# One assignment product per block with both centroid parts, first-unit maxima of three heads as b + relu(a - b), duplicates on GpSimd, and a new order

## The chip, the cores and the metric

One core of a Trainium2 chip runs the kernel. The metric is the device time of one execution in microseconds (us). The engines are TensorE (PE; its weight loads are listed as PEld), VectorE (DVE), ScalarE (ACT), GpSimd (POOL) and SyncE (SP), which issues DMAs.

## What is computed

Clustered attention for 4 batches x 8 heads x 768 tokens of 64 dimensions, with its output fed to a mixture of experts with greedy, capacity-limited routing. Cut to what matters here:

```python
q_assign = np.argmax(np.einsum('bhsd,hcd->bhsc', q_n, c_n), axis=-1)   # 16 centroids per head
k_assign = np.argmax(np.einsum('bhsd,hcd->bhsc', k_n, c_n), axis=-1)
mask = q_assign[:, :, :, None] == k_assign[:, :, None, :]
scores = scale * np.matmul(q, k.transpose(0, 1, 3, 2))
scores = np.where(mask, scores, -1000000000.0)
scores = scores - np.max(scores, axis=-1, keepdims=True)
attn = np.exp(scores); attn = attn / (np.sum(attn, axis=-1, keepdims=True) + 1e-09)
out = np.matmul(attn, v)                                               # then _moe_ref(x = out)
```

## The kernel before

Attention runs over eight units, `u = 0..7`; a unit is one batch and four heads, and has 24 blocks of 128 tokens (six per head). All inputs are held as two float16 parts, high and low, so that float16 products give nearly float32 precision. A unit goes through these steps, whose names stand in the order:

- `load`, `split_sc`, `split_hi`, `split_lo`: inputs arrive by DMA and are split into parts; `dup` copies the high parts into a second layout (`qb`, `kb`); `trans` (DMA) or `pt` and `ptc` (TensorE and a copy, first unit only) transpose the blocks into `qat`, `kat`, `qbt`, `kbt`.
- `cent` (L666) multiplies each block of queries or keys with the 16 centroids of its head, through `assign` (L655): for each block a product with the centroids' high part and one with their low part, 16 columns each, added up in a PSUM tile of the pool `pmx`. `hot0` to `hot5` make the one-hot marks of the nearest centroid from it. For the first unit `cent0` and `hh0` to `hh5` do the same, a head at a time.
- `m_mm` (L770): for a block of 128 queries the scores against the 768 keys of the head, high parts and marks alone, two products of 384 columns (L774); `m_rd` (L777) takes the maximum of each row on VectorE, one 128x768 reduction (L778). `row0` to `row2` put the maxima into `qbt`.
- `b_mm` (L812): the full scores, transposed, four products of 384 columns (L813, L817); `b_exp` (L819) the exponential on ScalarE; `res` (L825) the low part of the exponential, on GpSimd (letter P) or VectorE (D).
- `av` (L840): the value products, three for each of six query blocks, 66, 64 and 66 columns (L850, L852, L831). One PSUM tile of the pool `pav` holds a head's sums; `out0`, `out1`, `out2` scale it (L860, L863, L871), `hi0` and `hi1` split the result (L879, L883), and only then may the next head's `av` start. In the second block of a head come six products with the mean of the values (L856).

`m_mm` of unit u + 1, `cent` of unit u + 2 and `b_mm` and `av` of unit u run interleaved. The PSUM pool `psc` has three buffers of two banks, which `m_mm`, `b_mm` and `pt` share; `pmx` and `pav` have one each.

The program is unrolled, and the string `ATT_ORDER` says in which order its steps are issued: each entry is a step's name and its arguments (`m_rd,3,16` is the row maximum of block 16 of unit 3). Each engine takes its instructions in this order. `wd` is a filler product, which keeps TensorE occupied at the start. A second string orders the mixture of experts.

## Time and profile before

| | |
|---|---|
| time, median of 3 runs | 678.08 us (677.74 to 678.26) |
| profiled execution: time | 679.02 us |
| profiled execution: span | 677.2 us, mean granted clock 0.979 |
| busy in the span: TensorE, VectorE, ScalarE, GpSimd | 651.9, 506.6, 422.2, 484.9 us |

The span is the time from the first to the last instruction of the program; the time of the execution contains some more around it. Busy times are unions of an engine's instructions. TensorE's matmuls are pipelined, so each is listed longer than the step from one to the next: the step is read from the starts.

### The profile page before, as it was taken

How to read it: one execution, taken by the hardware profiler on the slowest of the kernel's cores; microseconds unless marked ns; L12 is line 12 of the kernel's file. 1: busy time of each engine (PE TensorE's matmuls, PEld its weight loads, DVE VectorE, ACT ScalarE, POOL GpSimd, SP SyncE). 2: the span in 40 equal slices, each digit the busy share in tenths (PEclk: the TensorE clock that was granted, in tenths of full speed). 3: DMA queues.
4: the chain of work that ended last, by engine and by line, in shares of the span. 5: the costliest groups of instructions: out<-in, count | busy, mean ns of one | idle time of the engine just before them, and what ended most of it. 6: DMA issues, size and time to landing. Idle time of an engine off the chain costs nothing. (4 is left out here: it accounts for less than half of the span.)

```text
span 677.2 us, 19763 instructions
## 1 busy us (share of the span) xinstructions
PE 651.9 (96%) x8286; PEld 436.9 (65%) x8286; DVE 506.6 (75%) x1157; ACT 422.2 (62%) x555; POOL 484.9 (72%) x389
## 2 busy tenths in 40 slices
PE   7999999999999999999999879999999999999996
PEld 5657777776777777777777559554545454545453
DVE  6898999999998989998887666877768585822020
ACT  8886676585767767565554046749494847598121
POOL 6568889899798877977774447677695949499301
PEclk9999999999999999999999569999999999999999
DMA  6887889776987979572223043729474766696101
GB/s 190 198 193 174 156 157 228 111 178 149 189 195 128 170 183 136 98 141 54 52 51 73 26 172 126 296 80 319 152 244 189 199 242 163 260 310 177 46 1 47
DMA packets 175451, 105.86 MB, mean 156 GB/s; under 512 B 135426, under 2 KB 160002, under 8 KB 175362
## 3 DMA queue, kind: packets, MB, share of 16 engines
q1 hardware_dynamic: 171378, 91.81, 56.7%
q0 software_dynamic: 3840, 12.59, 4.9%
q8 instruction: 65, 1.06, 0.6%
q10 hardware_dynamic: 144, 0.20, 0.1%
q14 instruction: 24, 0.20, 0.1%
HBM read 58.77 MB, written 12.58 MB: 105 GB/s over the span
## 5 line engine op out<-in xcount | busy, mean ns | idle before, releaser
L828 POOL TENSOR_TENSOR rt<-pt 128x768 f16<-128x768 f32 x176 | 267.2, 1544 | 63.5 <-ACT pt L820 63.3
L820 ACT ACTIVATE pt<-sc 128x768 f32<-128x768 f32 x192 | 150.6, 811 | 102.1 <-PE sc L817 99.2
L778 DVE TENSOR_REDUCE mxs<-sc 128x1 f32<-128x768 f32 x192 | 178.8, 951 | 12.7 <-PE sc L774 11.0
L1426 PE MATMUL pf<-xgt,w1h 128*128 128x384 f16 (+1 forms) x640 | 128.8, 293 | 0.3 <-DVE xgt L738 0.3
L850 PE MATMUL av<-vh,pt 128*128 128x66 f16 x1152 | 121.7, 194 | 0.1
L831 PE MATMUL av<-vh,rt 128*128 128x66 f16 x1152 | 121.4, 193 | 0.0
L852 PE MATMUL av<-vl,pt 128*128 128x64 f16 x1152 | 121.4, 191 | 0.0
L850 PEld LDWEIGHTS <-pt 128*128 128x128 bf16 x1152 | 106.0, 97 | 8.3
L852 PEld LDWEIGHTS <-pt 128*128 128x128 bf16 x1152 | 105.5, 98 | 8.5 <-issue 0.5
L831 PEld LDWEIGHTS <-rt 128*128 128x128 f16 x1152 | 104.7, 97 | 0.0
L813 PE MATMUL sc<-qbt,kbt 99*128 99x384 f16 x384 | 93.8, 325 | 1.1 <-DMA qbt<-mt 0.4
L817 PE MATMUL sc<-qat,kat 128*128 128x384 f16 x384 | 93.7, 325 | 0.0
L774 PE MATMUL sc<-kbt,qbt 80*128 80x384 f16 x384 | 90.2, 325 | 1.7 <-ACT qbt L736 0.6
L1426 PE MATMUL pf<-xgt,w1l 128*128 128x384 f16 (+1 forms) x320 | 90.0, 293 | 0.0
L1388 ACT ACTIVATE wr<-wr 128x1024 f32<-128x1024 f32 x64 | 66.8, 1046 | 26.4 <-DMA wr<-in_moe_w_dram 26.3
L1426 PEld LDWEIGHTS <-w1h 128*128 128x128 f16 x640 | 57.3, 97 | 28.7 <-issue 1.1
L1464 PE MATMUL pf<-w2h,hh 128*128 128x512 f16 x184 | 69.6, 378 | 0.0
L1464 PE MATMUL pf<-w2h,hl 128*128 128x512 f16 x184 | 69.4, 378 | 0.0
L1464 PE MATMUL pf<-w2l,hh 128*128 128x512 f16 x184 | 69.4, 378 | 0.0
L1398 POOL TENSOR_TENSOR w2l<-wr,w2h 128x1024 f16<-128x1024 f32 x32 | 67.6, 2134 | 1.9 <-ACT w2h L1391 1.6
L1398 POOL TENSOR_TENSOR w1l<-wr,w1h 128x1024 f16<-128x1024 f32 x32 | 67.6, 2138 | 0.2
L1402 POOL DMA_INDIRECT xg<-xrow,idx x24 | 23.3, 972 | 57.7 <-DVE idx L1361 20.6
(253 smaller groups left out, 1158.5 us busy)
## 6 DMA issues: line engine op xcount, KB each, us to landing
wr<-in_moe_w_dram SPq DMA_DIRECT2D x64, 512.0 KB
ld<-in_v_dram SPq DMA_DIRECT2D x8, 768.0 KB
xrow<-xb SPq DMA_DIRECT2D x16, 384.0 KB
ld<-in_k_dram SPq DMA_DIRECT2D x7, 768.0 KB
...
xg<-xrow,idx POOLq DMA_INDIRECT x24, 6.0
```

Of the source, the lines that this page charges most:

```text
L774: nc.tensor.matmul(p[:, half, :S // 2], QBT[u][:D + C, i, :], KBT[u][:D + C, h * J + half * 3:h * J + half * 3 + 3, :], start=True, stop=True)
L778: nc.vector.tensor_reduce(mxs[u % 3][:, i:i + 1], MP.pop((u, i))[:, :, :S // 2], axis=AX.XY, op=OP.max)
L813: nc.tensor.matmul(ps[:, half, :S // 2], KBT[u][:ER + 3, s, :], QBT[u][:ER + 3, cs, :], start=True, stop=False)
L817: nc.tensor.matmul(ps[:, half, :S // 2], KAT[u][:, s, :], QAT[u][:, cs, :], start=False, stop=True)
L820: nc.scalar.activation(pts[(u * 12 + s // 2) % RP][:, s % 2], MP.pop((u, "b", s))[:, :, :S // 2], AF.Exp, scale=ESC)
L828: (nc.vector if e == "D" else nc.gpsimd).tensor_sub(rts[x][:, s % 2], p.rearrange("p a b -> p (a b)"), hi_view(pts[x])[:, s % 2])
L831: nc.tensor.matmul(o[:, j, :], r[:, j * P:(j + 1) * P], VH[u][:, s, :], start=False, stop=(s % J == J - 1), skip_group_check=True)
L850: nc.tensor.matmul(o[:, j, :], hi[:, js], VH[u][:, s, :], start=(kt == 0 and j == 0), stop=False, skip_group_check=True)
L852: nc.tensor.matmul(o[:, j, :D], hi[:, js], VL[u][:, s, :], start=False, stop=False, skip_group_check=True)
L1398: nc.gpsimd.tensor_sub(lo, wrs[c], hi)
L1426: nc.tensor.matmul(o, (w1l if i == 2 else w1h)[x][:, c, fs], xgt[x][:, h + int(i == 1), ts], start=(first and i == 0), stop=(last and i == ...
L1464: nc.tensor.matmul(PS["o", p, g], (hl if i == 2 else hh)[x][:, f, g * P:(g + 1) * P], (w2l if i == 1 else w2h)[x][:, f, :], start=(f == 0 ...
```

## The change

1. `cent` issues one product for each block, 32 columns, against both parts of the centroids at once, into a tile of `psc`. The two results are added afterwards: `small` (`hotb` in the order) copies the low part's results to `cb` on ScalarE, and `both` (`hota`) adds the high part's to it on VectorE, into the tile of `pmx`. This holds for units 1 to 7, queries and keys; `cent0` stays.
2. In unit 0 the maxima of heads 1 to 3 (18 blocks) are made otherwise. `kd` subtracts the second half of a head's keys from the first; the first of the two products then gives a - b, where a and b are the scores against the two halves. `m_rl` takes relu(a - b) on ScalarE, and `m_rd` adds b and takes the maximum in one instruction of VectorE over 384 columns.
3. Six of the duplications of unit 0 run on GpSimd. The chain that normalises the centroids (`c2`) has ten steps instead of sixteen.
4. Value products write 65 columns instead of 66.
5. `ATT_ORDER` is new. As many fillers stand in it as before. The order of the mixture of experts is unchanged.

```diff
@@ -19,169 +19,174 @@
 ATT_ORDER = """
...
+m_rd,3,0 b_mm,2,10 row2,2,1 m_mm,3,1 out0,2,0 b_exp,2,10 cent,4,k,0 out1,2,0 cent,4,k,1 m_rd,3,1 cent,4,k,2 tab,11
+xtr,1,1 cent,4,k,3 res,2,7,P m_mm,3,2 hotb,4,k out2,2,0,D b_mm,2,11 hota,4,k hi0,2,0 res,2,9,P m_rd,3,2 b_exp,2,11
...
     def cent(u, name, h):
         if h == 0:
+            PC["w", name] = psc.tile([P, T, 2, C], F32, name="sc")
+        if h == 1:
             PC[name] = pmx.tile([P, T, C], F32, name="mx")
-        assign(PC[name][:, h * J:(h + 1) * J], (QAT if name == "q" else KAT)[u], u % NG, h, h == 0)
+        o, src, g = PC["w", name], (QAT if name == "q" else KAT)[u], u % NG * HG + h
+        for j in range(h * J, (h + 1) * J):
+            nc.tensor.matmul(o[:, j], src[:, j, :], ct[:, :, g * C:(g + 1) * C], start=(j % 16 == 0), stop=True,
+                             skip_group_check=True)
+
+    def small(u, name):
+        nc.scalar.activation(cb, PC["w", name][:, :, 1], AF.Copy)
+
+    def both(u, name):
+        nc.vector.tensor_tensor(PC[name], PC.pop(("w", name))[:, :, 0], cb, op=OP.add)
...
-            nc.tensor.matmul(p[:, half, :S // 2], QBT[u][:D + C, i, :],
-                             KBT[u][:D + C, h * J + half * 3:h * J + half * 3 + 3, :], start=True, stop=True)
+            x = KBT[u][:D + C, h * J + half * 3:h * J + half * 3 + 3, :]
+            if paired(u, i) and half == 0:
+                x = kdv(h)
+            nc.tensor.matmul(p[:, half, :S // 2], QBT[u][:D + C, i, :], x, start=True, stop=True)
+
+    def paired(u, i):
+        return u == 0 and i >= 1 * J
...
+    def kd(u, h):
+        k = KBT[u][:D + C, h * J:(h + 1) * J, :]
+        nc.vector.tensor_sub(kdv(h), k[:, 0:3], k[:, 3:6])
+
+    def m_rl(u, i):
+        nc.scalar.activation(rlv(i), MP[u, i][:, 0, :S // 2], AF.Relu)
...
-        nc.vector.tensor_reduce(mxs[u % 3][:, i:i + 1], MP.pop((u, i))[:, :, :S // 2], axis=AX.XY, op=OP.max)
+        o, p = mxs[u % 3][:, i:i + 1], MP.pop((u, i))
+        if paired(u, i):
+            nc.vector.tensor_tensor_reduce(rlv(i), p[:, 1, :S // 2], rlv(i), 1.0, LOWEST,
+                                           op0=OP.add, op1=OP.max, accum_out=o)
+        else:
+            nc.vector.tensor_reduce(o, p[:, :, :S // 2], axis=AX.XY, op=OP.max)
...
-            nc.tensor.matmul(o[:, j, :], hi[:, js], VH[u][:, s, :], start=(kt == 0 and j == 0), stop=False,
+            nc.tensor.matmul(o[:, j, :D + 1], hi[:, js], VH[u][:, s, :D + 1], start=(kt == 0 and j == 0), stop=False,
```

The instructions' order at two places. First VectorE, where unit 2's first head ends and unit 4's keys are assigned; before the change (`rc`, `av`, `xb` are the scaling and splitting of the head's sums, `mxs` row maxima of unit 3, `cmx` the first step of the marks):

```order
L778 TENSOR_REDUCE mxs_140<-sc 128x1
L860 TENSOR_SCALAR rc<-av 128x6
L863 RECIPROCAL rc<-rc 128x6
L871 TENSOR_TENSOR av<-av,rc 128x6x64
L778 TENSOR_REDUCE mxs_140<-sc 128x1
L883 TENSOR_TENSOR xb_146<-av,xb_146 128x6x64
L778 TENSOR_REDUCE mxs_140<-sc 128x1 x2
L679 TENSOR_REDUCE cmx<-mx 128x24
```

After it, where `mx<-sc,cb` (L691) is the sum of the two parts:

```order
L824 TENSOR_REDUCE mxs_140<-sc 128x1
L906 TENSOR_SCALAR rc<-av 128x6
L909 RECIPROCAL rc<-rc 128x6
L824 TENSOR_REDUCE mxs_140<-sc 128x1
L917 TENSOR_TENSOR av<-av,rc 128x6x64
L691 TENSOR_TENSOR mx<-sc,cb 128x384
L824 TENSOR_REDUCE mxs_140<-sc 128x1
L929 TENSOR_TENSOR xb_146<-av,xb_146 128x6x64
L824 TENSOR_REDUCE mxs_140<-sc 128x1
L701 TENSOR_REDUCE cmx<-mx 128x24
```

A row maximum now stands between L909 and L917, and the sum between L917 and the next maximum, so L929, the last step of the head's sums, is two instructions further from the first.

Second ScalarE, around its first exponential (`pt<-sc`, behind a table load); before (`vh` is a part of unit 1's values, `qb` and `kb` with 24x64 its duplicates and with 24x16 its marks, `kb` with 6x16 marks of unit 0, `qbt` transposed blocks of unit 0):

```order
L638 ACTIVATE vh_107<-ld_76 128x24x64
L695 ACTIVATE kb<-ceq 128x6x16
L736 ACTIVATE qbt_118<-sc 128x768
L736 ACTIVATE qbt_118<-sc 3x768
L650 ACTIVATE qb<-qa 128x24x64
L820 ACT_TABLE_LOAD
L820 ACTIVATE pt_127<-sc 128x768
L695 ACTIVATE kb<-ceq 128x24x16
L652 ACTIVATE kb<-ka 128x24x64
```

After, where L816 is a relu of unit 0 and L688 the copy of the low part's results of unit 1's queries:

```order
L816 ACTIVATE xt_149<-sc 128x384
L661 ACTIVATE qb<-qa 128x24x64
L758 ACTIVATE qbt_118<-sc 3x768
L816 ACTIVATE xt_148<-sc 128x384
L816 ACTIVATE xt_149<-sc 128x384
L688 ACTIVATE cb<-sc 128x384
L816 ACTIVATE xt_148<-sc 128x384
L717 ACTIVATE kb<-ceq 128x24x16
L816 ACTIVATE xt_149<-sc 128x384
L663 ACTIVATE kb<-ka 128x24x64
L866 ACT_TABLE_LOAD
L866 ACTIVATE pt_127<-sc 128x768
```

Four relus and a copy now stand between the duplicate of unit 1's queries and the table load, and unit 1's marks and duplicate of the keys moved ahead of the first exponential.

## Rows read from the trace of the kernel before

**Rows 1.** Five stretches: busy time, instructions, clock, DMA share, GB/s.

```profile
core 0: us, PE busy (x) PEld busy (x) DVE busy (x) ACT busy (x) POOL busy (x), PEclk, DMA share, GB/s
0.00:18.50 18.50, 14.54 (x139) 9.07 (x140) 12.11 (x43) 15.65 (x27) 13.40 (x36) 1.00 0.59 175
18.50:51.40 32.90, 30.75 (x351) 20.63 (x348) 30.85 (x52) 28.36 (x38) 19.66 (x10) 1.00 0.89 204
51.40:306.30 254.90, 251.94 (x4393) 191.25 (x4392) 238.69 (x388) 170.24 (x222) 216.88 (x161) 1.00 0.80 160
306.30:370.30 64.00, 64.00 (x1155) 48.83 (x1153) 51.88 (x90) 36.15 (x52) 44.84 (x31) 1.00 0.28 55
370.30:677.20 306.90, 290.63 (x2260) 167.15 (x2256) 173.05 (x588) 171.82 (x219) 190.13 (x153) 0.95 0.52 168
```

**Rows 2.** Groups by line, TensorE, 0 to 51.4: busy, mean ns, idle before.

```profile
L664 PE MATMUL av<-onesh 128*128 128x384 f16 x91 | 22.4, 360 | 1.5 <-POOL onesh L572 1.5
```

**Rows 3.** Waits of TensorE, 51.4 to 306.3: total us, times, longest.

```profile
PE mx L657 <- DVE L L954: 1.4, 2, 1.0
```

**Rows 4.** Waits of VectorE, 51.4 to 306.3.

```profile
DVE mxs L778 <- PE sc L774: 6.7, 16, 0.9
DVE xb L883 <- ACT xb L879: 2.2, 5, 0.7
```

**Rows 5.** Timeline of TensorE at a head boundary: start, us, instruction.

```profile
188.72 0.49 PE L774 MATMUL sc<-kbt,qbt 80*128 80x384 f16 x2
189.06 0.49 PE L813 MATMUL sc<-qbt,kbt 99*128 99x384 f16 x2
...
189.71 0.75 PE L657 MATMUL mx<-ct,kat 128*128 128x16 f16 x24
190.31 0.48 PE L774 MATMUL sc<-kbt,qbt 80*128 80x384 f16 x2
...
192.22 0.19 PE L850 MATMUL av<-vh,pt 128*128 128x66 f16 x1
```

**Rows 6.** Timeline of VectorE at the same boundary.

```profile
189.26 0.15 DVE L860 TENSOR_SCALAR rc<-av 128x6 f32<-128x6 f32 x1
...
189.67 0.57 DVE L871 TENSOR_TENSOR av<-av,rc 128x384 f32<-128x384 f32 x1
190.15 0.95 DVE L778 TENSOR_REDUCE mxs<-sc 128x1 f32<-128x768 f32 x1
191.01 0.55 DVE L883 TENSOR_TENSOR xb<-av,xb 128x384 f16<-128x384 f32 x1
191.48 0.95 DVE L778 TENSOR_REDUCE mxs<-sc 128x1 f32<-128x768 f32 x1
```

**Rows 7.** Timeline of TensorE in the second half: a 32-column product.

```profile
443.20 0.31 PE L1202 MATMUL pc<-oh,ind 128*128 128x32 bf16 x6
```

**Rows 8.** Timeline of TensorE: value products, first and last of ten.

```profile
196.37 0.19 PE L850 MATMUL av<-vh,pt 128*128 128x66 f16 x1
...
196.64 0.19 PE L850 MATMUL av<-vh,pt 128*128 128x66 f16 x1
```

**Rows 9.** Groups by line and shape, VectorE, 0 to 374.

```profile
L828 DVE TENSOR_TENSOR rt<-pt 128x768 f16<-128x768 f32 x16 | 15.8, 999 | 3.4 <-ACT pt L820 3.3
...
L528 DVE TENSOR_TENSOR ss<-ss 128x1 f32<-128x1 f32 x4 | 0.6, 160 | 0.1
```

**Rows 10.** Groups by line and shape, VectorE, 372 to 450: compare with accumulator.

```profile
L1236 DVE TENSOR_SCALAR_CACHE_REDUCE scr<-pc 32x8 bf16<-32x8 f32 x12 | 1.9, 156 | 3.6 <-PE pc L1230 2.0 <-PE pc L1196 1.5
...
L1236 DVE DVE_READ_ACCUMULATOR scr<-pc 32x1 bf16 x12 | 0.9, 74 | 0.0
```

**Rows 11.** Groups by line and shape, ScalarE, 0 to 374.

```profile
L879 ACT ACTIVATE xb<-av 128x384 f16<-128x384 f32 x32 | 15.6, 488 | 11.7 <-DVE av L871 8.7 <-PE sc L817 2.4 <-issue 0.3
...
L650 ACT ACTIVATE qb<-qa 128x384 f16<-128x384 f16 x4 | 2.0, 511 | 0.0
```

**Rows 12.** Groups by line and shape, GpSimd, 0 to 374.

```profile
L645 POOL TENSOR_TENSOR ka<-ld,ka 128x384 f16<-128x384 f32 x3 | 2.7, 917 | 3.3 <-ACT ka L638 3.3
...
L569 POOL MEMSET qm<- 128x600 f16 x1 | 0.6, 600 | 0.0
```

More of the change, by code (lines that the diff above doesn't have):

```diff
@@ L182 @@
[L182 to L184 removed]
+load,0,q,0,A ones tab,0 wd ident split_hi,0,q,0,D tab,4 wd load,0,k,0 tab,10 wd zqb loadc wd load,0,q,1 wd wd load,0,k,1
+zkb wd load,0,q,2 wd load,0,k,3 wd wd split_hi,0,k,0,D load,0,k,2 misc wd c0 dup,0,k,0 load,0,v,- wd c1 load,0,q,3 wd
@@ new lines @@
+av,0,1 m_rl,0,21 m_mm,0,22 vact,1 m_rd,0,20 res,0,6,P av,0,2 vh2,1 trans,2,ka,- m_rd,0,21 m_rl,0,22 b_mm,0,7 m_rd,0,22
+av,0,3 b_exp,0,7 row0,0,2 res,0,4,D m_mm,0,23 pt,0,qm,2 m_rl,0,23 b_mm,0,8 res,0,7,P ptc,0,qm,2,A m_rd,0,23 av,0,4 vl2,1
+b_exp,0,8 m_mm,1,0 load,2,v,- m_mm,1,1 split_hi,2,q,-,D m_rd,1,0 b_mm,0,9 res,0,8,P load,3,q,- av,0,5 m_rd,1,1 b_mm,0,10
+b_exp,0,9 out0,0,0 row1,0,3 row0,0,3 out1,0,0 m_mm,1,2 tab,1 out2,0,0,D b_exp,0,10 res,0,9,P cent,2,k,0 cent,2,k,1
+cent,2,k,2 m_rd,1,2 cent,2,k,3 hi0,0,0 b_mm,0,11 hotb,2,k hi1,0,0 res,0,10,P m_mm,1,4 hota,2,k b_exp,0,11 av,0,6
@@ new lines @@
+m_rd,1,9 av,0,13 split_hi,2,v,-,D m_mm,1,12 hot4,2,k res,0,18,P av,0,14 m_rd,1,10 b_mm,0,19 hot5,2,k m_rd,1,12 av,0,15
+b_exp,0,19 b_mm,0,20 row0,1,0 row1,1,0 split_lo,2,v,-,D split_hi,3,k,-,D rowt,1,0 b_mm,0,22 m_mm,1,13 av,0,16 b_exp,0,20
+m_rd,1,13 res,0,19,P av,0,17 b_exp,0,22 lg0,0,0 out0,0,2 row2,1,0 m_mm,1,14 out1,0,2 lg1,0,0 cent,2,q,0 out2,0,2,D
+res,0,20,P cent,2,q,1 cent,2,q,2 load,4,k,- cent,2,q,3 m_rd,1,14 hi0,0,2 b_mm,0,23 trans,2,kb,- hotb,2,q b_mm,0,21
+b_exp,0,23 tab,3 hi1,0,2 res,0,22,P hota,2,q av,0,18 b_exp,0,21 hot0,2,q m_mm,1,15 av,0,19 tab,2 hot1,2,q res,0,21,P
@@ new lines @@
+split_hi,3,q,-,D m_rd,1,22 b_mm,1,7 vl2,2 av,1,3 b_exp,1,7 row0,1,1 row1,1,1 b_mm,1,8 split_lo,3,q,-,D rowt,1,1 av,1,4
+b_exp,1,8 av,1,5 m_mm,2,0 res,1,7,P out0,1,0 b_mm,1,9 out1,1,0 m_rd,2,0 row2,1,1 m_mm,2,1 b_exp,1,9 res,1,8,P m_rd,2,1
+b_mm,1,10 load,4,v,- xst,0,0 m_mm,2,2 out2,1,0,D b_exp,1,10 cent,3,k,0 cent,3,k,1 trans,3,qa,- cent,3,k,2 m_rd,2,2
+res,1,6,P cent,3,k,3 hi0,1,0 b_mm,1,11 hotb,3,k hi1,1,0 m_mm,2,4 hota,3,k b_exp,1,11 res,1,10,P av,1,6 m_rd,2,4
+split_hi,3,v,-,D m_mm,2,6 m_mm,2,3 m_rd,2,6 b_mm,1,13 res,1,9,P av,1,7 hot0,3,k b_exp,1,13 m_rd,2,3 av,1,8 res,1,11,P
@@ new lines @@
+row2,3,1 b_mm,3,10 out0,3,0 m_rd,4,1 cent,5,k,0 load,6,k,- cent,5,k,1 b_exp,3,10 cent,5,k,2 res,3,6,P cent,5,k,3
+out1,3,0 xst,2,0 b_mm,3,11 out2,3,0,D hotb,5,k trans,5,qa,- m_mm,4,2 hi0,3,0 hota,5,k b_exp,3,11 res,3,7,P hi1,3,0
+m_mm,4,4 m_rd,4,2 b_mm,3,13 res,3,8,P m_rd,4,4 m_mm,4,6 b_exp,3,13 av,3,6 m_rd,4,6 dup,5,k,- m_mm,4,3 av,3,7 res,3,10,P
+hot0,5,k av,3,8 m_rd,4,3 b_mm,3,12 res,3,11,P hot1,5,k m_mm,4,5 b_exp,3,12 av,3,9 m_rd,4,5 b_mm,3,14 res,3,13,P
+load,6,v,- hot2,5,k b_mm,3,15 b_exp,3,14 load,6,q,- hot3,5,k m_mm,4,7 res,3,12,P b_exp,3,15 av,3,10 hot4,5,k m_mm,4,9
@@ new lines @@
+xst,3,0 m_mm,5,2 hota,6,k hi0,4,0 res,4,8,P trans,6,qa,- b_exp,4,10 m_rd,5,2 b_mm,4,11 m_mm,5,3 hi1,4,0 b_exp,4,11
+m_mm,5,4 res,4,9,P m_rd,5,3 av,4,6 dup,6,k,- av,4,7 m_rd,5,4 res,4,10,P b_mm,4,12 hot0,6,k m_mm,5,6 b_exp,4,12 av,4,8
+m_rd,5,6 b_mm,4,13 res,4,12,P hot1,6,k m_mm,5,5 b_exp,4,13 b_mm,4,14 hot2,6,k m_rd,5,5 res,4,11,P m_mm,5,7 b_exp,4,14
+av,4,9 hot3,6,k b_mm,4,15 m_rd,5,7 res,4,13,P av,4,10 b_exp,4,15 m_mm,5,9 hot4,6,k av,4,11 m_rd,5,9 res,4,15,P b_mm,4,16
+load,7,k,- out0,4,1 m_mm,5,8 out1,4,1 b_exp,4,16 out2,4,1,D b_mm,4,17 res,4,14,P m_rd,5,8 hi0,4,1 lg0,3,1 b_mm,4,18
@@ L185 @@
+bb,1,9 bb,1,4 bb,1,10
 """
```

350 lines of the change are left out of this document (168 added, 182 removed).

## The prediction

> **What bounds the kernel now.** I read the stretches first: busy time of each engine in five parts of the span, cut at the first row-maximum product (18.5 us), the first value product (51.4), the first value product of the seventh unit (306.3) and the last value product (370.3). The reader is to see [rows 1] that from 51.4 to 306.3 TensorE is busy 251.9 of 254.9 us and VectorE 238.7, so TensorE is the limit with VectorE close behind (16.2 us free); that from 306.3 to 370.3 TensorE is busy throughout and VectorE has 12 us free; and that behind 370.3 lies the mixture of experts, which the change does not touch. Before 51.4 it is otherwise: 91 of TensorE's products there are fillers that compute nothing [rows 2], 91 x 0.16 = 14.7 us of array time at the step of a 384-column product (0.33 us for two, [rows 5]). TensorE waits there for the data that VectorE and ScalarE prepare; between 18.5 and 51.4 they are busy 30.9 and 28.4 of 32.9 us [rows 1].
>
> Then the waits. In the long stretch TensorE's longest named wait adds up to 1.4 us [rows 3], while VectorE waits 6.7 us for row-maximum products alone [rows 4]. So there a product taken from TensorE shortens the kernel, as long as VectorE, which gets work, does not use up its slack.
>
> **Term 1, the assignment products.** Each of 14 groups (queries and keys of units 1 to 7) has 24 blocks; before, two 16-column products with a weight load each, 48 in all; after, 24 products of 32 columns. The timeline shows 24 of the old in 0.60 us, start to start (189.71 to 190.31, [rows 5]), 25 ns each, so 48 take 1.20 us. A 32-column product with a weight load exists in the second half: six last 0.31 us together and one 0.177, so (0.31 - 0.177) / 5 = 27 ns a step [rows 7]. 24 x 25 or 27 ns is 0.60 or 0.64 us: a group saves 0.56 to 0.60, and I take 0.60. Unit 1's two groups lie in the start, where TensorE has fillers to spare: nothing. The other 12 lie between 51.4 and 306.3: **-7.2 us** (bounds -6.7 and -7.2).
>
> **Term 2, 65 columns for 66.** Two of three value products and the 192 with the means lose a column: 2 x 1152 + 192 = 2496 products. Nine value products, three of each kind, take 0.27 us (196.37 to 196.64, [rows 8]), so 90 ns for 66 + 64 + 66 columns: the step follows the columns, with some 3 ns on top. The granted clock is 1.00 up to 370.3 [rows 1], the upper of the two levels, 2.4 GHz, and a column is 0.42 ns: **-1.0 us**. No row has an odd width, so the bounds are -1.0 and nothing, and I could not exclude a loss of the same size; I take -1.0, since nothing in the rows makes parity matter.
>
> **Term 3, what VectorE gets.** Each group now needs a sum of the two parts (hota) on VectorE, 128x384 of float32 from PSUM. The nearest rows are the scaling and the low part of the output, also 128x384: 0.57 and 0.55 us long, the next instruction 0.48 and 0.47 us behind their start [rows 6]. Twelve in the long stretch: 12 x 0.47 = 5.6 us. In front of it stands a copy on ScalarE (0.49 us, [rows 11]), which is busy 170 of 254.9 us there and hides it; but the sum waits for the copy. Four of the new maxima also lie in this stretch and give back 4 x 0.3 (below). The order moves some steps across the stretch's ends (a split in; a residual, a maximum and short ones out), by my estimate -1.7 us. VectorE then has 238.7 + 5.6 - 1.2 - 1.7 = 241.4 us of work in a stretch that TensorE could pass in 254.9 - 8.0 = 246.9: 5.5 us free where it had 16.2.
>
> The price is paid at the head boundaries. There the one accumulator for values must be read out (out0, out1, out2, copy, hi1) before the next head's products start. Before, out0 to hi1 with one row maximum between ran from 189.26 to about 191.56, 2.3 us [rows 6], while TensorE had 3.50 us of other products (188.72 to 192.22, [rows 5]); assignment products were 1.2 us of that. The VectorE excerpt of the order shows one more maximum (0.86 us) and the sum (0.47) inside this chain: 3.6 us, and with the 0.5 us between TensorE's last value product and out0 (188.72 to 189.26) 4.1. The new order lays beside it two score blocks (2 x 0.65, 189.06 to 189.71), five pairs of maximum products (5 x 0.33) and 0.60 of assignment products, together 3.55 us. So 0.5 us of waiting there. Also the products of a group now sit in one of the three score buffers until the sum is done, where before they sat in a buffer of their own. The other boundaries in the order are better covered, so I take 0.2 us for each of the 12, between nothing and the whole 0.6 that it saved: **+2.4 us** (0 to 7.2).
>
> **Term 4, the start.** The 18 new maxima: a step of a 951 ns maximum is 0.86 us (190.15 to 191.01, [rows 6]). The new one reads half as much: between 0.47 (the 128x384 step) with 0.09 for reading the accumulator, 0.56, if it goes like the sums, and 0.86, no gain. A compare with accumulator lasts 0.156 and its read 0.074 [rows 10], so the read is cheap, and I take 0.56: 18 x 0.30 = 5.4 us off VectorE. Six small steps of the centroid chain go as well, 0.16 us each [rows 9], 1.0 us. Against that VectorE gets two sums (0.9), three differences of keys (80x384, at most 0.5 each: 1.4) and three residuals that GpSimd made (0.99 each, [rows 9]: 2.6 at the step of a maximum). Sum: -5.4 - 1.0 + 0.9 + 1.4 + 2.6 = -1.5 us. ScalarE gets 18 halves for the relu and two copies, some 0.49 us each [rows 11]: +9.8, and loses six duplications of 0.51 [rows 11]: -3.1. In the ScalarE excerpt of the order relus stand in front of the first exponential. The six duplications on GpSimd take between 0.6 (a fill of 600) and 0.92 us (a 128x384 subtraction) each [rows 12]; GpSimd is busy 33 of the first 51.4 us [rows 1] and covers them. So ScalarE, busy 44 of the first 51.4 us, gets about 6.7 us that it has little room for, and VectorE loses 1.5. The start may be shorter by 1.5 or longer by 2; I take **0**.
>
> **Sum.** -7.2 - 1.0 + 2.4 + 0 = -5.8 us. The profiled execution took 679.0 us, a span of 677.2 and 1.8 around it, 0.9 above the median of 678.1. Counted from the median: **672.3 us**.
>
> **Rivals.**
> - *Everything is hidden and the start gets shorter.* VectorE's named waits in the long stretch [rows 4] then shrink without touching TensorE: -8.2, and -1.5 from the start: 668.4. For it speaks that TensorE lost only 3 us in the stretch with VectorE busy 94%; against it that the slack falls to a third.
> - *VectorE takes over the bound, and the kernel is slower.* Place: 51.4 to 306.3. If VectorE stays idle as long as now, 16.2 us, because its waits come from the chain through TensorE and ScalarE and not from spare time, the stretch takes 241.4 + 16.2 = 257.6, 2.7 us more than now; less 0.2 for the columns in the last stretch: 680.6. It decides from 13.5 us of idle time on (254.9 - 241.4). Against it: much of that idle time was waiting for TensorE [rows 4], which now comes sooner. The Trainium skill bears on this ("VectorE: DVE Perf Modes", section "The DRAIN you can't avoid"): the next operation does not start until the pipe is empty. By that the sums would cost their whole 0.57 us, 6.8 instead of 5.6, and 4.3 us would stay free. The rows differ: the maximum of 190.15 lasts 0.95 us and the next instruction starts at 191.01, 0.09 us before its end, so I count steps.
> - *The new maximum is dear.* If its step is over 0.56 + 5.8 / 18 = 0.88 us, the start gives back all the rest: 678 at 0.88, 680 at 1.0. No row shows this instruction.
> - *The wider product does not halve the time,* because a group spread over two banks of PSUM steps slower: at 50 ns a product term 1 is nothing, and 678.1 - 1.0 + 2.4 is 679.5. The 27 ns of [rows 7] speak against it.
>
> **Chances.** The forecast 0.58; the first rival 0.17; VectorE's bound 0.12; the dear maximum 0.10; the last 0.03. A measurement of this kernel can tell about 0.2%, 1.4 us, from no change. The first two cases are faster throughout; of the next two, half lies above the bound, a third within it and the rest below. So faster 0.79, same 0.10, slower 0.11. Range: from 667.5, a little beyond the first rival, to 678.5, which leaves out the slower half of the two dear cases.
>
> **What would show it.** In the changed kernel's trace: assignment products at 25 to 27 ns a step; nine value products in under 0.27 us; the long stretch 249 us instead of 254.9, with TensorE idle about 5 us and VectorE 8; the new maximum with its read under 0.6 us a step; the first value product near 51 us. I am wrong if VectorE is idle over 13 us in that stretch, if a score product waits over 0.5 us for the buffer at each group, or if the first value product comes after 54 us.

## The result and the profile after

The changed kernel is slower: median 683.38 us (681.30 to 685.48, 8 runs) against 678.77 for the kernel before beside it (677.74 to 681.75, 8 runs), ratio 1.0067 with an interval of 1.0048 to 1.0086. The forecast was 672.3. The profiled execution took 685.48 us, a span of 683.7 at a mean granted clock of 0.971 (before: 677.2 and 0.979). It is the slowest of the eight: its trace shows 6.5 us more than the trace of before, where the medians differ by 4.6, and what the other seven had less of is not recorded.

The same five stretches as in [rows 1], cut at the same events of the changed kernel's trace (first row-maximum product 21.7, first value product 59.9, seventh unit 311.1, last value product 377.0). Two of the cuts of [rows 1] are not quite what they are called: the first row-maximum product of the kernel before starts at 17.55 and the one at 18.5 is the second block's, so that the first one now comes 4.1 us later; and both cuts at the last value product lie 0.7 us ahead of the very last ones (371.0 and 377.7).

```profile
0.00:21.70 21.70, 15.17 (x138) 9.34 (x139) 11.94 (x34) 13.52 (x23) 14.85 (x42) 0.84 0.58 184
21.70:59.90 38.20, 32.21 (x302) 20.64 (x303) 30.58 (x77) 33.27 (x50) 17.63 (x12) 0.96 0.70 158
59.90:311.10 251.20, 247.88 (x4104) 184.09 (x4102) 238.01 (x397) 178.80 (x239) 219.72 (x155) 1.00 0.80 160
311.10:377.00 65.90, 64.69 (x1158) 49.05 (x1156) 52.68 (x92) 36.45 (x52) 46.97 (x35) 1.00 0.24 58
377.00:683.70 306.70, 290.47 (x2260) 167.10 (x2256) 172.73 (x588) 171.92 (x219) 189.92 (x153) 0.95 0.52 168
```

The first value product comes at 59.9 instead of 51.4 us: the start loses 8.5 us, and its clock column shows 0.84 and 0.96 where it showed 1.00. From the first to the last value product it takes 317.1 instead of 318.9 us, a gain of 1.8 where 5.8 were forecast. The mixture of experts is 0.2 us shorter. 8.5 - 1.8 - 0.2 = 6.5 us, the difference of the two spans.

**The start.** Stretch by stretch (columns as in [rows 1]; the third number from the end is the clock):

```profile
5.70:9.40 3.70, 0.36 (x6) 0.35 (x6) 2.34 (x10) 3.62 (x8) 3.10 (x11) 1.00 1.03 365
9.40:16.20 6.80, 4.74 (x49) 3.22 (x47) 4.87 (x11) 2.53 (x6) 5.90 (x10) 0.50 0.51 148
16.20:36.70 20.50, 17.86 (x231) 12.43 (x230) 16.99 (x43) 17.57 (x26) 11.25 (x7) 1.00 0.57 127
36.70:40.10 3.40, 3.40 (x27) 2.30 (x24) 1.95 (x6) 2.87 (x4) 0.00 (x0) 0.50 0.99 171
40.10:59.90 19.80, 16.36 (x125) 9.78 (x124) 15.95 (x40) 17.13 (x26) 7.47 (x5) 1.00 0.70 182
```

For 10.2 us in two stretches TensorE runs at the lower level, 1.2 GHz; the kernel before shows 1.00 in every stretch up to its last value product [rows 1]. Ahead of the first fall TensorE had nothing to do (its timeline; the number in brackets is the idle time before the row):

```profile
5.15 0.52 PE L675 MATMUL av<-onesh 128*128 128x384 f16 x1
9.04 0.52 PE L754 MATMUL sc<-ident,ka 128*128 128x128 f16 x6 [3.37 <-DVE ss L534]
```

L675 is the last of the 14 fillers that the new order puts ahead of the first transposition of keys; one more stands between it and the copy of the centroids (`c4`). The order before had 11 and 9 there. Ahead of the second fall are two idle times of 1.04 and 0.93 us, at 33.1 and 35.2.

**Short VectorE steps that end with a GpSimd instruction.** VectorE's timeline at the end of the centroid chain, and GpSimd's at the same time:

```profile
9.01 0.86 DVE L534 TENSOR_SCALAR sq<-cf,ss 128x64 f32<-128x64 f32 x1
9.90 1.00 DVE L534 CAST cst<-sq 128x128 f16<-128x128 f32 x1
...
10.94 0.91 DVE L534 TENSOR_TENSOR cst<-sq,cst 128x128 f16<-128x128 f32 x1
```

```profile
8.91 0.91 POOL L652 TENSOR_TENSOR ka<-ld,ka 128x384 f16<-128x384 f32 x1
9.78 0.91 POOL L652 TENSOR_TENSOR qa<-ld,qa 128x384 f16<-128x384 f32 x1
10.63 0.20 POOL L1032 MEMSET wdig<- 128x128 bf16 x1
10.79 0.91 POOL L652 TENSOR_TENSOR qa<-ld,qa 128x384 f16<-128x384 f32 x1
```

The first ends at 9.87, the GpSimd instruction beside it at 9.82; the third at 11.85 and 11.70. In the kernel before, with GpSimd idle there, the first took 0.26 us, and the other two, half as wide (128x64), 0.19 and 0.22. The longest is the second copy of the first head's maxima:

```profile
39.31 0.16 DVE L842 TENSOR_SCALAR qm<-mxs 128x12 f16<-128x12 f32 x1
40.13 0.56 DVE L760 COPY kbt<-sc 128x768 f16<-128x768 f16 x1 [0.66 <-PE sc L754]
40.61 2.88 DVE L838 TENSOR_SCALAR qm<-mxs 128x12 f16<-128x12 f32 x1
```

```profile
40.48 2.98 POOL L652 TENSOR_TENSOR vl<-ld,vh 128x1536 f16<-128x1536 f32 x1 [6.03 <-ACT vh L645]
```

Two steps of the same shape: 0.16 us with GpSimd idle, 2.88 us beside a GpSimd instruction that ends at 43.46. The Trainium skill ("GPSIMD Engine Reference", section "Key points") says that GpSimd shares its SBUF interfaces with VectorE, and names as contending those VectorE instructions that run in a two-port mode or have two SBUF inputs. The trace agrees for the second kind: the step of 10.94 us, with two inputs in SBUF, was held, and the new maximum of 54.11 us, with one operand in PSUM, ran its usual 0.56 us beside a GpSimd residual of 53.77 to 55.23. In which mode the held steps with one input ran, no view shows.

**The long stretch.** One group of assignment products in TensorE's timeline, and the new maximum in VectorE's:

```profile
278.48 0.75 PE L684 MATMUL sc<-ct,kat 128*128 128x32 f16 x24
279.18 0.48 PE L859 MATMUL sc<-qbt,kbt 99*128 99x384 f16 x2
```

```profile
46.00 0.55 DVE L821 CUSTOM_DVE_ANT_0 xt<-sc,xt 128x384 f32<-128x384 f32 x1
46.47 0.08 DVE L821 DVE_READ_ACCUMULATOR2_ANT mxs<- 128x1 f32 x1
46.47 0.55 DVE L821 CUSTOM_DVE_ANT_0 xt<-sc,xt 128x384 f32<-128x384 f32 x1
```

The 24 products take 0.60 us (0.70 start to start, of which 0.10 is a wait for the next score buffer), a new maximum 0.47 with its read beside the next one. The named waits of TensorE in 59.9 to 311.1 still look small:

```profile
PE sc L684 <- DVE mxs L824: 1.1, 1, 1.1
PE sc L859 <- DVE mx L691: 0.4, 2, 0.2
PE sc L799 <- ACT pt L866: 0.3, 1, 0.3
PE sc L799 <- DVE mx L691: 0.3, 1, 0.3
```

But this view counts a wait only once the product ahead has ended, and a product is listed some 0.2 to 0.3 us beyond its step. So I summed the starts instead: for each line of TensorE the distance from one start to the next, and as a wait all of it that is over 20 ns above the median of that line. From the first to the last value product, in us:

| | before | after | e9 (old assignment, new order; below) |
|---|---|---|---|
| assignment products, waits taken out | 14.5 | 7.3 | 14.5 |
| waits | 6.0 | 11.4 | 11.8 |
| - ahead of score products and transpositions | 3.9 | 7.0 | 5.9 |
| - ahead of value products | 0.4 | 2.6 | 2.3 |
| - ahead of assignment products | 1.7 | 1.9 | 2.0 |
| - steps made longer by a fall of the clock | 0 | 0 | 1.6 |
| all other products | 298.4 | 298.4 | 298.3 |
| together | 318.9 | 317.1 | 324.6 |

The products save 7.2 us, to the tenth what was forecast, and 5.4 of it comes back as waits. Of these, 3.1 us lie ahead of score products, behind a score buffer that VectorE or ScalarE has not yet read, and 2.2 at head boundaries, ahead of the next head's value products; there a single wait, at 374.0 behind three routing steps of VectorE, is 1.2. The mean step of some 3,430 value products, waits taken out, is 29.9 ns before and after.

### The profile page after: what moved, and what is told of

It is laid out like the page before. It is cut to its first block, busy times and chain, and to the rows that moved or that the text cites. A ratio compares the mean times of both kernels' runs of the same rounds, so it can differ in the third digit from the quotient of the medians.

```text
span 683.7 us, 19177 instructions
## 1 busy us (share of the span) xinstructions
PE 650.4 (95%) x7950; PEld 430.2 (63%) x7950; DVE 505.9 (74%) x1186; ACT 434.0 (63%) x581; POOL 489.1 (72%) x395
## 3 DMA queue, kind: packets, MB, share of 16 engines
q1 hardware_dynamic: 171378, 91.81, 54.9%
## 5 line engine op out<-in xcount | busy, mean ns | idle before, releaser
L824 DVE TENSOR_REDUCE mxs<-sc 128x1 f32<-128x768 f32 x174 | 161.7, 951 | 11.7 <-PE sc L799 11.1
L896 PE MATMUL av<-vh,pt 128*128 128x65 f16 x1152 | 122.8, 194 | 1.2 <-DVE xb L929 1.1
L877 PE MATMUL av<-vh,rt 128*128 128x65 f16 x1152 | 122.4, 193 | 0.2 <-issue 0.2
L799 PE MATMUL sc<-kbt,qbt 80*128 80x384 f16 x366 | 87.5, 325 | 1.3 <-ACT pt L866 0.3
L1444 POOL TENSOR_TENSOR w1l<-wr,w1h 128x1024 f16<-128x1024 f32 x32 | 67.5, 2135 | 0.3
```

The lines of the kernel that those rows point to most:

```text
L799: nc.tensor.matmul(p[:, half, :S // 2], QBT[u][:D + C, i, :], x, start=True, stop=True)
L824: nc.vector.tensor_reduce(o, p[:, :, :S // 2], axis=AX.XY, op=OP.max)
L877: nc.tensor.matmul(o[:, j, :D + 1], r[:, j * P:(j + 1) * P], VH[u][:, s, :D + 1], start=False, stop=(s % J == J - 1), skip_group_check=True)
L896: nc.tensor.matmul(o[:, j, :D + 1], hi[:, js], VH[u][:, s, :D + 1], start=(kt == 0 and j == 0), stop=False, skip_group_check=True)
L1444: nc.gpsimd.tensor_sub(lo, wrs[c], hi)
```

## The experiments

All are timed in 5 rounds beside the kernel before. "First" is the first value product of the profiled execution, "from there" the time to the last one.

| run | median us | ratio to before (interval) | first | from there |
|---|---|---|---|---|
| before | 678.0 to 678.8 | 1 | 51.4 | 318.9 |
| after | 683.38 | 1.0067 (1.0048 to 1.0086) | 59.9 | 317.1 |
| x1_old_start | 684.07 | 1.0086 (1.0060 to 1.0111) | 51.2 | 324.5 |
| x2_new_start | 690.58 | 1.0197 (1.0164 to 1.0231) | 56.4 | 326.3 |
| x3_wide_only | 701.03 | 1.0333 (1.0305 to 1.0360) | 53.6 | 341.3 |
| x4_relu_only | 687.54 | 1.0146 (1.0121 to 1.0172) | 59.1 | 320.5 |
| e5_row_first | 682.59 | 1.0064 (1.0045 to 1.0082) | 58.5 | 317.1 |
| e6_fillers | 680.82 | 1.0041 (1.0022 to 1.0061) | 54.9 | 319.9 |
| e7_old_first_17us | 679.69 | 1.0039 (1.0021 to 1.0058) | 55.1 | 316.8 |
| e8_old_start_fixed | 683.05 | 1.0081 (1.0064 to 1.0099) | 51.2 | 322.6 |
| e9_old_cents | 689.32 | 1.0144 (1.0118 to 1.0170) | 55.9 | 324.6 |
| e10_best_start | 679.05 | 0.9999 (0.9985 to 1.0013) | 54.1 | 316.8 |
| e11_65_columns | 678.16 | 0.9984 (0.9966 to 1.0002) | 51.3 | 318.7 |
| e12_old_maxima | 680.39 | 1.0022 (1.0006 to 1.0039) | 54.5 | 317.2 |
| f1_fillers_row | 680.05 | 1.0022 (1.0009 to 1.0034) | 55.0 | 316.8 |
| f2_best | 679.56 | 1.0019 (1.0005 to 1.0033) | 54.1 | 319.7 |
| f3_best_no_relu | 681.03 | 1.0033 (1.0022 to 1.0044) | 55.3 | 317.5 |
| f4_before_table | 677.99 | 0.9991 (0.9975 to 1.0008) | 51.1 | 318.3 |

In the profiled executions of x1, x2, x3, x4, e6, e9 and f2 the clock also fell between the first and the last value product, so their "from there" contains such a fall. In e6 and f2 a wait stands ahead of it. In e6 two copies of row maxima were held by GpSimd, then TensorE waited for a step queued behind them:

```profile
246.86 3.53 DVE L845 TENSOR_SCALAR m<-mxs 128x24 f16<-128x24 f32 x1
247.28 3.17 DVE L841 TENSOR_SCALAR m<-mxs 128x24 f16<-128x24 f32 x1
```

```profile
247.43 2.88 POOL L877 TENSOR_TENSOR rt<-pt 128x768 f16<-128x768 f32 x2
```

```profile
250.53 0.49 PE L802 MATMUL sc<-kbt,qbt 80*128 80x384 f16 x2 [1.75 <-DVE L L1003]
```

In f1 the same two copies took 0.56 and 0.21 us. From 251.0 to 254.4 the clock of e6 was 0.50, and the steps there were 1.4 us longer: with the wait, the 3 us that e6 and f2 (where the same happened) take more than f1 "from there".

**Which half lost the time: x1 and x2.** The order of before up to the second unit's first row maximum and the steps of the change behind it, with the old forms of what stands ahead; and the reverse.

```diff
     def paired(u, i):
-        return u == 0 and i >= 1 * J
+        return False
     def cent(u, name, h):
+        if not (u > 1):
...
```

> The changed kernel with the start of the kernel before: its order up to the second unit's first row maximum, its chain for the centroids, its maxima and its duplicates; the wider assignment products (units 2 to 7), the 65 columns and the new order stay behind that point. If the start is what lost the time, the first value product comes at 51 us again, the stretch from there to the seventh unit takes about 251 us, and the whole is 2 to 5 us under the kernel before (674 to 677). Rival, the rest of the change gains nothing by itself and the changed kernel's short long stretch (251.2 us) is only work that its start had already done: then the long stretch goes back to 254 or 255 us and the time is that of the kernel before or more (678 to 681).

> The reverse: the changed kernel's start (new chain, relu maxima, duplicates on GpSimd, its order, and unit 1's groups with the wider product) with the order of before behind the second unit's first row maximum, and the old assignment of units 2 to 7. If the start loses the time, the first value product comes at 58 to 61 us, a stretch of the lower clock level is seen before 45 us, and the kernel is 5 to 9 us slower than before (683 to 687). Rival, the start pays back what it costs because more of unit 1's work is done when it ends: then the time is within 2 us of the kernel before (677 to 681).

Both times lie above both of their ranges. Neither told what it was built for, because the place where the two orders are joined (the seam) costs as much as what was sought. In x1 the start is that of before, and then VectorE stands still:

```profile
57.20 0.33 DVE L560 TENSOR_SCALAR wg<-wgf 128x32 f16<-128x32 f32 x1
57.57 5.86 DVE L561 SCALAR_TENSOR_TENSOR wg<-wgf,wg 128x32 f16<-128x32 f32 x1
63.46 1.82 DVE L829 TENSOR_REDUCE mxs<-sc 128x1 f32<-128x768 f32 x2
```

```profile
56.86 0.81 POOL L1037 MEMSET wdig<- 128x128 bf16 x5
57.65 5.73 POOL L879 TENSOR_TENSOR rt<-pt 128x768 f16<-128x768 f32 x4
```

The step of 128x32, 0.19 us elsewhere, ended with the last of four GpSimd residuals that ran one behind the other without a gap, at 63.38. TensorE then waited 4.45 us for the row maximum queued behind it, and its clock was 0.50 from 64.3 to 71.1 us. In x2 a load of unit 2's values comes too late at the seam, TensorE waits 3.7 us at 65.5, and its clock was 0.50 from 67.5 to 77.8. By the same sum of starts, the waits of x2 outside that wait and its falls are those of the kernel before: 3.9 us ahead of score products, 0.4 ahead of value products. What x2 does show is that the new start is late with the old order behind it too (56.4), and x1 that the old start is in time with the new forms behind it.

**The wider product and the maxima, each alone in the old order: x3 and x4.**

```diff
-cent,2,k,3 hot0,2,k
+cent,2,k,3 hotb,2,k hota,2,k hot0,2,k
```

> The wider assignment product alone, in the order of before: the copy and the sum stand right behind each group of products; value products write 66 columns again, and the start is that of before but for unit 1's two groups. By the prediction's terms 1 and 3 the long stretch loses 7.2 us of products and gets 0 to 7.2 back: 671 to 678 us, most likely 673 to 675. Rival, the sum on VectorE costs as much as it saves where the order was not rearranged for it, since a group now holds one of the three score buffers until the sum is done: waits of TensorE for the sum of 0.5 us at each group, and 678 to 682 us.

```diff
-hh1,2 m_mm,0,7
+hh1,2 kd,0,1 m_mm,0,7
-wd m_rd,0,6 wd
+wd m_rl,0,6 m_rd,0,6 wd
```

> The first unit's maxima of three heads as b + relu(a - b) alone, in the order of before, with three differences of keys ahead of them; everything else is as before. VectorE loses 18 x 0.38 = 6.8 us (a step of 0.48 for one of 0.86) and gets three differences (about 1.4); ScalarE gets 18 x 0.49 = 8.8 us. If the new maxima help the start, the first value product comes 1 to 4 us before 51.4 and the time is 675 to 678. If each maximum now waits for its relu behind other work on ScalarE, the first value product comes after 53 us, with waits of the maximum for the relu of over 3 us in all, and the time is 680 to 684. If neither limits the start, it is within 1 us of the kernel before.

x3 is worse than its rival: TensorE's and VectorE's waits from 53.6 to 331 us have the sum and its copy in them, and TensorE's clock falls between 150 and 250 us (0.90 from 150 to 200, 0.97 from 200 to 250).

```profile
DVE mx L692 <- ACT cb L689: 12.0, 11, 2.1
PE sc L800 <- DVE mxs L825: 5.3, 9, 1.0
PE sc L860 <- DVE mxs L825: 4.5, 7, 1.4
PE sc L685 <- DVE mxs L825: 2.3, 2, 1.9
```

So the wider product needs another order: with copy and sum right behind it, a group keeps one of the three score buffers while VectorE waits for the copy, 12 us in all. In x4 each maximum waits for its relu behind the exponentials and the long copies on ScalarE (10.4 us in 9 waits from 30 to 60 us), the clock is 0.84 on average from 37.8 to 59.1, and the second outcome of its text is what came, with 687.5 us above its 680 to 684. A second fall, from 177.2 to 180.7, stands in the long stretch of this profile.

**Single causes in the changed kernel: e5 to e8.**

```diff
-row1,0,0 ptc,0,kb,3,D wd wd load,2,q,- row0,0,0 wd
+row1,0,0 row0,0,0 ptc,0,kb,3,D wd wd load,2,q,- wd
```

> The changed kernel with one small VectorE step moved: the second of the two copies of the first head's row maxima (128x12, 0.16 us elsewhere) stands right behind the first, 0.8 us earlier, and so ahead of the time in which GpSimd computes the low part of unit 1's values (40.48 to 43.46 us); in the changed kernel it took 2.88 us and ended with that GpSimd instruction. If GpSimd holds VectorE back there, the step takes 0.16 us, the transposition behind it starts 2 us earlier, the first value product comes 1.5 to 2.5 us before 59.9 and the time is 1 to 2.5 us under the changed kernel (681 to 682.5). Rival, the step's length is only where another wait shows: then the wait moves to the next VectorE step, and the time stays within 0.7 us of the changed kernel (683.4).

The first value product came 1.4 us earlier and the median is 0.8 lower, just short of what was expected: the step took its short time, but the clock fell once more behind it, at 50 to 55 us (0.70), after the same two falls as in the changed kernel:

```profile
5.00:10.00 5.00, 1.29 (x9) 0.56 (x6) 3.02 (x11) 4.88 (x11) 4.30 (x14) 0.86 0.97 324
10.00:15.00 5.00, 3.49 (x38) 2.38 (x39) 3.28 (x7) 1.85 (x4) 5.00 (x9) 0.50 0.41 153
35.00:40.00 5.00, 4.76 (x48) 3.31 (x49) 3.34 (x11) 3.60 (x7) 0.41 (x1) 0.66 0.98 174
50.00:55.00 5.00, 5.00 (x28) 2.94 (x26) 2.23 (x7) 4.16 (x7) 4.05 (x4) 0.70 0.52 99
```

The executions of this one kernel differ by the clock, too: the two at a mean of 0.980 took 681.1 us, the three at 0.970 took 683.0.

```diff
-c2,6 pt,0,ka,0
+c2,6 wd wd wd wd wd wd wd wd wd wd wd wd wd wd wd wd pt,0,ka,0
-c2,9 c3
+c2,9 wd wd wd wd wd wd c3
```

> The changed kernel with 22 more filler products: 16 in the gap of 3.4 us before the first keys are transposed and 6 behind the transposition of the first queries, where TensorE had 1.4 and 0.6 us of nothing. If the lower clock level (9.4 to 16.2 us) is what makes the start late, the clock stays at its upper level there, and the time is 2 to 4 us under the changed kernel (679.5 to 681.5). Rival, TensorE waits for VectorE's centroid chain there and a faster clock only makes it wait longer: the clock stays up, the first row-maximum product comes no more than 1 us before 21.7, and the time is within 1 us of the changed kernel (682.4 to 684.4).

The clock stayed at 1.00 throughout the start, the second fall did not come either, and the first value product came at 54.9: 5.0 of the 8.5 us. The first row-maximum product came 1.5 us earlier, so the rival fails. But the 5.0 us are not the clock alone. The second copy of the first head's maxima, which was not moved here, now came ahead of GpSimd's long instruction (37.94 us) and was not held:

```profile
37.66 0.16 DVE L841 TENSOR_SCALAR qm<-mxs 128x12 f16<-128x12 f32 x1
```

For e7 the order of before stands up to its first assignment product, with its chain of sixteen steps (three fillers more than the changed kernel):

```diff
-load,0,q,0,A ones tab,0 wd ident split_hi,0,q,0,D tab,4 wd load,0,k,0 tab,10 wd zqb loadc wd load,0,q,1 wd wd load,0,k,1
+ident load,0,q,0,A split_hi,0,q,0,D ones load,0,k,0 wtio wd loadc wd tab,0 misc wd tab,4 load,0,k,3 wd load,0,k,2 wd
...
```

> The order and the chain of before up to the first assignment product (about 11 us), and the changed kernel from there on. If 3 to 4 of the 8.5 us are lost in the centroid chain (late square root, last steps stretched to 0.9 to 1.0 us by GpSimd) and the lower clock beside it, the first row-maximum product comes at 18 to 19 us instead of 21.7 and the time is 3 to 4 us under the changed kernel (679 to 681). Rival, what bounds the rest of the start are ScalarE's relus and the order of the middle part: then the 3 us are waited for again before the first value product, which still comes after 58 us, and the time is 682 to 684.

The first value product came at 55.1 and the first row-maximum product at 19.4, a little behind its 18 to 19; the time is at the low end. Here too the clock is up until 46.2 us, where it falls for 3.4.

```diff
-vl2,1 tab,10 tab,14 tab,8 tab,12 wgs tab,15 res,0,6,P
+vl2,1 res,0,6,P
-row1,1,0
+row1,1,0 wgs
```

> As the run with the old start, but the step that splits the gate's weights (128x32, which took 5.86 us there beside four GpSimd residuals one behind the other, where it takes 0.19 elsewhere) stands after unit 1's first head again, and five table steps of GpSimd are spread out. If that one step cost the 4.5 us of TensorE's idle time and the lower clock behind it (65 to 72 us), 7 to 8 us come back: 675 to 677.5. Rival, the seam between the two orders costs by itself, whatever VectorE does: 680 to 684. By the prediction's terms 1 to 3 with an untouched start it would be 672 to 673; by the waits for score buffers that the changed kernel's trace shows (4.1 us more in units 1 to 6, 1.3 at the end) 676 to 678.

Moving the step brought 3.1 us of the stretch that it held up back (46.0 for 49.1 us from the first value product to the second unit's), not 7 to 8: two other short steps, the copies of the fourth head's maxima, now took 0.77 and 1.51 us beside GpSimd's residuals, with 2.4 us of waiting on TensorE behind them. The rival, that the seam costs by itself, is nearer.

**The disputed terms: e9 to e12,** all but e11 on e7.

```diff
-cent,2,k,3 hi0,0,0 b_mm,0,11 hotb,2,k hi1,0,0 res,0,10,P m_mm,1,4 hota,2,k
+cent,2,k,3 hi0,0,0 b_mm,0,11 hi1,0,0 res,0,10,P m_mm,1,4
```

> The kernel with the first 17 us of before (679.7 us) and the old assignment of units 1 to 7: two products of 16 columns for each block into a buffer of their own, no copy and no sum; the order is otherwise the same. By the prediction's terms 1 and 3 the wider product saves 7.2 - 2.4 = 4.8 us, so this kernel is about 4.8 us slower (684 to 685). Rival, what TensorE saves it waits for at the score buffers, which a group holds until VectorE's sum is done: then the waits of the score products shrink by 3 to 4 us here, and the time is within 2 us of 679.7, above or below.

Its median is 9.6 us above e7's (about 7 by the ratios to the kernel before), beyond both outcomes. The third column above says why: the assignment products cost their 7.2 us again, and the waits are 11.8 although no group holds a score buffer and no sum stands on VectorE. Not all of the 11.8 is waiting: the clock fell from 132.4 to 135.9 us.

```profile
130.00:140.00 10.00, 8.86 (x179) 7.63 (x180) 6.94 (x12) 3.87 (x6) 6.63 (x6) 0.83 1.09 185
```

Without the 1.6 us of longer steps there, 10.2 are left, against 11.1 in e7 and 6.0 before. Ahead of score products 1.1 us less is waited than in e7 (5.9 for 7.0), so about 1 us goes with the sums and the held buffer; the 2.3 ahead of value products stay as they are. So some 4 of the 5 us came with the order, not with the sums. (0.8 us more are lost before the first value product and 1.1 behind the last.)

```diff
-hh4,0,k pt,0,qa,2
+hh4,0,k wd wd wd wd wd wd wd wd wd wd pt,0,qa,2
...
-m_rl,0,14 b_mm,0,1
+m_rl,0,14 wd wd wd wd wd wd wd wd b_mm,0,1
```

> The kernel with the first 17 us of before, the second copy of the first head's maxima right behind the first, and 23 more fillers in three gaps of TensorE (10 before the transposition of the queries' block group 2, 5 before the first transposed marks of group 2, 8 before the second score block). If what is left of the late start there (55.1 for 51.4 us) is the lower clock at 45 to 50 us and the short VectorE step that GpSimd holds up, the first value product comes at 52.5 to 54 us, no fall of the clock is seen before 300 us, and the time is 677 to 678.5. Rival, the relus and ScalarE's long copies set that part: 55 us again, and 679 to 680.

The first value product came at 54.1 us, and the clock did not fall before 374 us. All that the change lost is won back, to the time of the kernel before beside it (678.79); 679.05 itself is 0.5 above the expected range.

```diff
-            nc.tensor.matmul(o[:, j, :], hi[:, js], VH[u][:, s, :], start=(kt == 0 and j == 0), stop=False,
+            nc.tensor.matmul(o[:, j, :D + 1], hi[:, js], VH[u][:, s, :D + 1], start=(kt == 0 and j == 0), stop=False,
```

> The kernel before with 65 for 66 columns in its value products and nothing else. By term 2 of the prediction 1.0 us faster (677.0 of 678.0). By the steps in the changed kernel's trace (29.9 ns a product with either) no difference: 677.7 to 678.4.

The interval (0.9966 to 1.0002) holds both no change and the forecast's microsecond, so the times can't tell. The profile can: the 0.3 us that it shows from the first to the last value product all lie in waits, and each kind of value product steps as before (the one that went from 66 to 65 columns on the exponential's low part 29.58 ns in both, the one of 64 columns 28.6). Nothing was gained by the last column.

```diff
-        return u == 0 and i >= 1 * J
+        return False
```

> The kernel with the first 17 us of before, and the old maxima for all of unit 0 (one 128x768 reduction each; no differences of keys, no relus); the order is otherwise the same. VectorE gets 18 x 0.38 = 6.8 us back and loses three differences (1.0 us); ScalarE loses 18 x 0.4 = 7.2 us. If the relus ahead of the exponentials on ScalarE make the middle of the start late, the first value product comes before 54 us and the time is 677 to 679. If VectorE is what the middle waits for, as the change supposes, it comes after 57 us and the time is 682 to 685. If neither, within 1 us of 679.7.

The first value product came at 54.5 against 55.1 us, the time is 680.4 against 679.7. From 17.5 to 51 us VectorE was busy 31.1 us here and 26.2 in e7, so the work that the old maxima brought back went into time in which it had been idle. But in e7 the clock fell at 46.2 us and here it did not, so this pair can't price the maxima. Against e10, which has no fall either but also has the moved step and the fillers, this run is 0.4 us later at the first value product and 1.3 us slower.

**Clock against chain, and short steps elsewhere: f1 to f4.**

f1 is the changed kernel with the edits of e5 and e6 and these:

```diff
-hh2,3 pt,0,qb,2
+hh2,3 wd wd wd wd wd pt,0,qb,2
-m_rl,0,14 b_mm,0,1
+m_rl,0,14 wd wd wd wd wd wd wd wd b_mm,0,1
```

> The changed kernel (its chain and its first order kept) with 35 more fillers in four gaps of TensorE before 51 us and the second copy of the first head's maxima behind the first. If the late start is the clock, which falls behind these gaps, and not the chain, the first value product comes at 53.5 to 55 us, as with the first 17 us of before (54.1), and the time is 678.5 to 680. If the chain's stretched steps matter by themselves, 56 to 57 us and 681 to 682.

With 35 fillers and the moved maxima step, and the new chain and first order kept:

```profile
5.70:9.40 3.70, 2.42 (x20) 1.41 (x19) 2.35 (x10) 3.63 (x8) 3.13 (x11) 1.00 0.99 340
9.40:16.20 6.80, 5.63 (x71) 3.88 (x69) 5.83 (x14) 2.80 (x7) 5.91 (x10) 1.00 0.48 155
16.20:36.70 20.50, 18.82 (x243) 13.18 (x241) 17.21 (x44) 18.89 (x29) 11.26 (x7) 1.00 0.57 140
36.70:40.10 3.40, 3.40 (x27) 2.18 (x26) 3.33 (x11) 3.38 (x4) 2.08 (x1) 1.00 0.83 175
40.10:55.00 14.90, 14.11 (x109) 8.42 (x108) 10.47 (x33) 14.50 (x23) 5.41 (x5) 1.00 0.90 221
```

Against the same rows of the changed kernel: the 6.8 and 3.4 us at 0.50 are at 1.00, and the first value product is 4.9 us earlier, at 55.0. The chain's three stretched steps are as long here (0.87, 1.01 and 0.90 us), so against e10 (54.1) the chain and the first order are worth 0.9 us. What the clock is worth is read against e5, which has the moved step as well and differs in the fillers alone: 58.5 to 55.0, 3.5 us of the start, and 1.0064 to 1.0022 of the time. The moved step by itself is the 1.4 us of e5 (59.9 to 58.5; 1.0067 to 1.0064 is too little to tell).

```diff
-tab,14 tab,8 tab,7 dup,0,q,1,P
+tab,14 tab,8 dup,0,q,1,P
-bb,0,8 bb,0,10 bb,0,9 av,7,14
+av,7,14
-res,7,20,P b_mm,7,23 hi1,7,2 b_exp,7,21
+res,7,20,P b_mm,7,23 hi1,7,2 bb,0,8 bb,0,10 bb,0,9 b_exp,7,21
```

The table step stands behind `m_rd,0,10` now. f3 is this with the edit of e12, and f4 the kernel before with the table step moved alone.

> The kernel with the first 17 us of before, the moved maxima step and the fillers (679.05 us), with two moves more: a table step of VectorE (128x16, which took 2.2 us at 10.2 us, beside GpSimd's fills, and held the first mark's step for 0.9) stands behind the 11th row maximum; three routing steps of VectorE (1.4, 0.2 and 2.0 us) stand behind the last but one head's result instead of ahead of it, where TensorE waited 1.2 us. If short steps that wait for GpSimd are the cause at both places, the first value product comes about 1 us earlier (53), the last stretch is 1.2 us shorter (26.4), and the time is 676.5 to 677.5. Rival, the waits only move on: 678.5 to 679.5.

> The same with the old row maxima for all of unit 0, no differences of keys and no relus. If the new maxima help once nothing else is late, it is 1 to 2 us slower than the kernel with them (678 to 679). If they cost as much on ScalarE as they save on VectorE, it is within 0.7 us of it, and the first value product comes at 52.5 to 53.5 us.

> The kernel before with one table step of VectorE (128x16) moved from 14.4 us, where it took 1.36 us beside two fills of GpSimd, to behind the 11th row maximum. If GpSimd held that step, and so the copy and the mark's step queued behind it, the step takes 0.15 us at its new place unless another GpSimd instruction runs there, the marks come 0.7 to 1.2 us earlier, and the time is 0 to 1 us under the kernel before (677.3 to 678.3). Rival, the copy behind it was held by itself: nothing changes in the first 17 us.

f2's rival holds: the table step was stretched no more and nothing came earlier (54.1), and TensorE's 1.2 us at the last head boundary but one became 0.8 at the next residual. f3 is 1.5 us slower than f2, so with the rest in order the new maxima do help (first value product 54.1 against 55.3); in f3, as in e12, a copy of maxima at 46.0 us was held to 1.0 us, and how much of the 1.2 is that was not separated. f4's first value product comes 0.3 us earlier, and its interval holds 1. A short step that GpSimd holds is thus worth something only where TensorE or the chain waits for it, as in e5 and x1.

No run beats the kernel before by more than its interval; e10 equals it.

## Why the prediction was wrong

- **Term 4, the start at 0, is the step that failed.** The start came 8.5 us later in the profiled execution. The term summed VectorE's and ScalarE's work and asked which engine would be full; both had idle time in the end (7.6 and 4.9 us of the 38.2 behind 21.7). I counted the 91 fillers of [rows 2] as 14.7 us of array time to spare and the change as leaving their number alone, and never asked where the new order puts them. 14 instead of 11 stand ahead of the first keys and 1 instead of 9 behind, so TensorE idled 3.4 us and ran at half its clock for 6.8 and later 3.4 us. Fillers alone bring back 3.5 us (f1 against e5). A short step that GpSimd held for 2.9 us, which the term had not either, is 1.4 (e5), the chain and the first order 0.9 (f1 against e10). The remaining 2.7 lie in the middle of the start and stay open. The relus that ScalarE has there ahead of exponentials and transposed copies are not shown to be the cause: without them the first value product came later, not earlier (e12 against e10, f3 against f2). That half of the 10.2 us at the lower clock is 5.1, and e6 gave 5.0 back, is luck: in e6 the held step went away as well.
- **Term 3 was mis-sized, and for another reason.** +2.4 was forecast, 5.4 us came as waits. At the head boundaries 2.2 came, close to the forecast, but not by its cause: e9 has the same 2.3 without any sum, and half of them is one wait behind routing steps. The other 3.1, at score products, had no price of their own in the term; about 1 of them goes with the sums and the held buffer (e9). The rest came with the order as a whole: scores, maxima and exponentials are interleaved so that each group finds room, and the three buffers run dry more often; x2, with the order of before in the long stretch, has the waits of before (x3 shows that the wider product without such an order is far worse). Which of its moves does it was not separated. My test for it, a wait of 0.5 us per group, looked at the wrong place: the waits at score products are 0.5 us or less, anywhere.
- **Term 1 was right:** -7.2 us measured, at 25 ns a product as forecast from [rows 7]. A statement of the Trainium skill ("TensorE: Matmul & The Clock Gate", section "Wait — 56ns, not 53.3ns?") fits: starts come no closer than about 25 ns however few the columns; 16 and 32 columns both step at 25 here.
- **Term 2 was 1.0 for nothing measurable.** The bound "nothing" was on paper, and I took the other end: a product of 65 columns steps like one of 66 (29.58 ns in e11 and before). The rows gave 90 ns for three products, too coarse for one column.
- **The new maximum** is cheaper than the 0.56 us assumed, 0.47 to 0.48, and still brought nothing that the first run shows; f3 against f2 puts it at up to 1.2 us of the start, once the rest is in order.
- **The rivals.** VectorE's bound came true in its sign (VectorE idle 13.2 us in the long stretch, and the stretch short of its gain) but the stretch did become shorter, by 3.7 us, so it is not why the kernel is slower. The dear maximum is refuted. Two of the three signs that I had set for being wrong appeared, the 13.2 us and a first value product after 54 us; the cause of the second was in none of the cases.
